# Another queue for the first piece of k, another order on GpSimd, and a new order table in a fused attention and MoE kernel

## The chip, the cores and the metric

The kernel runs on one core of one Trainium2 chip. The metric is device time in microseconds (us) of one execution. Before the change the median of 3 runs is 299.79 us (299.76 to 300.42).

## The reference

Sliding-window attention with ALiBi bias, followed by a layer of two matrix products with g = h cos(h) between them:

```python
q, k, v: (8, 8, 576, 64) float32          # batch, heads, sequence, head_dim
scores = q k^T / 8 - slope_h |i - j|      # kept where 0 <= i - j < 128, else -1e9
attn = exp(scores - max); attn /= sum(attn)
x = (attn v) transposed to (4608, 512)
h = x @ w_in                              # w_in (512, 2048)
out = (h * cos(h)) @ w_out                # w_out (2048, 512), out (4608, 512) float32
```

## The kernel before, in words

**Tiles and stages.** The 4608 tokens are nine chunks of 512. For each batch of the attention there are nine units: two halves of 256 queries for each of four pairs of heads, and one unit for the 64 tokens of the tail. A unit runs scores (PE, L539 and L529), exps (ScalarE, L598 and L590), a multiplication by a mask that holds the bias (VectorE, L623 and L611), P times V (PE, L653/L656 and L640/L642), the division by the row sum (VectorE, L694 to L712), and a transpose of the result into xT, on PE (L742, copied by L752/L753) or by a DMA. A chunk of the MoE part runs the first product (L782 for most chunks; L975 for chunk 0, in halves; L876 for the last chunks, which use Strassen-like sums of quarters), cos on ScalarE (L787, L980, L940), the multiplication on VectorE (L791, L984), and the second product (L1161 for chunk 0, L1067 and L1138 for the others). The loop over chunks mixes the units of later batches with the products of earlier chunks.

**What sets the order.** Every operation is recorded by `op` (L115) with the keys that it reads and writes, a due priority and assumed durations (`occ` for the engine, `lat` to its result). The order is not worked out in the kernel: `TABLE` (L30) is a packed list of the operations' numbers, one after the other, with a bit that picks ScalarE or VectorE for operations that may run on either. `follow` (L160) reads it and `emit` (L174) writes each engine's program in that order and adds the semaphore waits that the keys ask for. Each engine, and the DMA queue that it issues to, then works strictly in its own order.

**The start.** Batch 0's q and k come in two pieces each, with 8 and 10 token rows a partition group (L344). `load_first_q` (L359) lets SyncE (SP) fetch q's first piece in float32, 512 KB, into the first two output buffers `ob`, from where VectorE (L367) and ScalarE (L368) cast one half each into `qB` (tile gsum). `load_qk` (L351) lets GpSimd (POOL) issue the other loads, cast to bfloat16 by the DMA (L356). `distances` (L425) fills `dif` on GpSimd with an iota and two selects; ScalarE makes the eight masks `EM` from it (L460), and VectorE copies a part of them (L465). `identity` (L419) is a memset and a select on GpSimd. `qk_transposes` (L469) transposes the rows on PE against the identity (L483) into PSUM, from where ScalarE (L500) or VectorE (L501) copies them into qt and kt. GpSimd's program begins: load k piece 1, iota, load q piece 2, two selects, load k piece 2, memset, select, then v (L375) and w_in (L407). The lines that record the start:

```python
load_first_q()
load_qk("k", k, 0, 0)
distances()
identity()
load_qk("q", q, 0, 1)
load_qk("k", k, 0, 1)
```

Of the kernel before, what the change touches and what calls it, by code (L numbers as in the profile page):

```python
# [27 lines left out]


TABLE = (  # L30
    'c-nPV2Y6If7JmPfH!Wo*A%PHdEHqifjs=k}tV#(GFqBXPBn4$bu`FK_%_4*%1ObV(K#D*JSt&-E!h-'
    '0xDvPKfD@{Z`QYO7kX6D^JciMYzU|;fHUhcd1+;jf_Kj&N_3_w#jJy552L+3%Pc;zlP#H-yktj(-'
    'pEjqM{ck}PJwCrB3q-'
    '{9M;&d$5qHR9WADS}~;_2H1xbO#`q+wdtgon`B>6%HyG|f?3%VnDsdnr<5N0St5ZZ)?8zmXNGD<Zg2=y6N`U+Gy?'
    '$F$*GyJWJoN!r+3anTS_iMU&FrmJy)q1{k##U*rYHRJHq^Dy35b!Y@oPU}o$A?_9;n<O%5Xs0l2&{m^^1BgNm_9P'
    '~pqObs4C1TN&{Qy{6(86~%nA#%H5NW^O=4`d2vLnc~h(_}2&mQcz_^`@$G{b79x#rnLjt-93Hcj0-'
    'yv%|m2e+*e0cZK}!+72b)WUaJT8@pXD+fk0N6bOV1gB(Si4?NA5T2-'
    '!JB(zEKr!Mj%{>;HUNYjab!Z7$qCql;L3G!CjefR+FFk(bw73vr<2ntCbb8MB)_5dQYyf6J%<J=0tY;ul(MgN&rc'
    'O0s&EiG$uIcm#Y~Vab;v#yqnaVrE7GY>V-A}Btqa`;P_Nv&jvF#{*7WM`>VMkre&#)Wy?uO_aV#gax-'
    'm{4=v5trFP6j>R?Tw2c0rY#J*M(j<PaOY>o)>#w^hUa2)xJ2kX>J~-'  # L40
    '#3SczLYEI#)13`0UMgZCvSU&r@KXVhQx8AYHOt^~S#t385v1pL)39f1&X4(!RY_VSn%~;N7Le~0Vt5k)3C!7qncH'
    'Sb_KKyP6<WQBL=(H{om`}^2hwehkBNkN1f6-'
    '=6Jf`#n1*9F&|{#~8ip5b`?XFO3>mnmKg4fqM&X#D2BXTu`vb#MxEL-'
    '2=FZh<=U!>)?uhVjo~ev?pC0h90j^d!W2#$W>Vg}3Lez;yMB~`dF58D5!*GHZ4bkokcrZJo8XMBIs3+J`c0!*&!='
    'cNak2M(+9t6%k<c;_TI5&xT-;_~SjMe)zLQ?kr-'
    '9G)}so_oZgT~!nS)>B%(>F{i(nL<%Kma6dPT_kIY8xqVGm@6sSZY)QY;}3kyZHF!JjrNbPWohF6A1kpQae^Jz>4Y'
    'nMq|4ag_#Z%abX$X0Qx{bdg5-'
    'w!C^Sy0wzSSv6YO*7!5g5KOZPW>L)jeqDWi^PVfHiNt_&bV&I7<#pb?el1f*R3lvbBscPqQM6(|M=#E!7MQtWiEo'
    '^$q8jetWg{{laSk`ID;w6<lHL!It@CI3ZRWxET-dy=6bdfZi^BN)-'
    'kx6rkxYh^Af7Y$CX%W0qP@nf!;+_cuy#JAV$$(>L5)aS8M@n1a32RRL3Yb{W0a`!VJ8|o4{JEnxs(L});p(&v8a9'  # L50
    'u_yO{KZHL$YuW?tu(Sy-'
    '!vCGTmAdZpg4wXLtycpkG<<E5@OtDZg=!_1h1+Njmjw*z0aL)7QnhFOPv(elHPlI>oe%EXgvk}suL+RHI+l!oPEe'
    'ttc)y)KY7q-'
    'GO9HpEp~!82*s>_!_J5TR{@5f%EL7h^Wh(4l4fbO%j~jd783&`#My06C4>3;+Is6L%3tT|^hYe#$tr1&iB&6{dwW'
    'wmj!;Baz_4=p8Jja_9ps>tY{=<;GUvOwSAXGq+K`;>!KNrH|ImXY(ASTzHFN^apdvpSj*r6^VK)$8H@P=`NPcPO&'
    'XkYSBhFw`irt0gqb!LQPqlVQC7VwU?z)4yP6n<)+6xUk=rH29r)HJ=#nkkufV0J5o_@v9wsQWd0@&P$WT0e*0vOC'
    'WIl=#9la*x}LDtWaQG=0xl2(#f%Kz3QWi+K|tR$xwKh#_K~ywPUk>V_~X988-'
    'dL$7M*|kTUzrMQ~>ttJm@GYT>9QFLiQ#JGHIu^Q5UX9joXGsV+1N~s5tf4rg&Z0t843@yK)VUZ;eO{vvf>bj#_<{'
    'E{YJE13lG{)N}UY3D6Y>lsCkRX4ja{$9_e$IQETy;j`zD56VwIGwJ{vRRhIkkY72;<?OL;WxyDsbjLJ`d?#gik4L'
    '%OwvOj>3X-Yk5pe`ia}jeHouYwjx-lYe?zUO*6w~{=z!E<7?VOdoJcyIBk3;YN22T&Udsl*?z2EoT*eN`VQ(2lOw'  # L60
    '$ie!%Cd#CND}y^H-5G~apWoVM#%(x$>q1=4UeA7@v$>FHVpXpRNz-`z1w9-2S&rNI|0<^yIkuIxJ1&2qr-'
    'yn-P&*BAkwbEg<YgZWM`B<Ux7!?;yxT0hEB9Poq9_H<xB+6$<+&1*V*jXQ=!i##UhbBC-HxJ9b4f>O5FQM$GVlYY'
    '0;EzOMeT$+Oi@ir?~G>em;QF`Fb7Uw0-'
    ')DSUv5QX5E;wvHsQX@ok50m+CO*%wR0XM0gH$JNq(o?|pd}rcrfU%@Ny^NS$EwY}9WNlRrb}CwAb0!CyUIkX8zeE'
    't`lBMNi5`Z9289jS-byN0#8`Z0-K46!6u51NJvfI*I<pVOKD}#Bep<(EjKAJ>#OvyA?}aT-'
    'Eb<QtZWG>gAiq@nZu|-Z>5YIIxXgTPJ-Qv8(%8OF{x~utj?J<T~4~q=Mu!G!`B%o{U^X7EYfMjy|cFw5l`KlR}P!'
    'Ka8_mW<8uzKs|eA|5Ic*_e7cdlcU3q+K^v!GU5I4-4igxj^A<ASLge=;<iQSZL!w7=WR?W#-'
    'vXhCLeN@7x(>g+{qRDABl6lLS<Fw>!h`LQKaFe(HMu)ipAva=P&;AW;|7_8}?>Xa&1&CWqRI3oTyJm0VHkMj~b-'
    'KU~R;VLVn(IO$x|2XD-#Cwa~YvoxGM@0FUnOnlZXB(9|3jhMQu{ARUV7(DVnyPJ@o)_f&pP-'
    '0v1&I@q5tK0fHEZqW2B6vpePz;Nsr3p!)OwvLraMQ%IB0%b!Fk8kvD!^ICX(d5SU`>)JBl;A)3x!^A~*gA1H!Njk'  # L70
    '9bb31AJ#9jLnSFn5nJP8V+>6WI*{{9$K=-'
    'Ii4(}ekB>9rlTbz8;dAV@$vsGY#Mm*p3)v9cI)0mEeyn;9Sk1Ej+_{IEB=6m(OWM%qp|L4FkV=POcUwRSz4?%tjO'
    '!EE7%nJVFo1y$1xLEKDW3+%V*`a_(LEi!<eA{Ja22J?)4@RI|7PRIIN8a6UkTIrQNx^0MmIX}Gdse33v8*ibI3(}'
    'Q6!`hQq7VFL0TWDyL%1z)LEb|Fqa2QJsRyz<9M$)jGC(Gyq6mu#GUiIyWiMn}lrw_vC^2CnX65Kq(JOA5auqsW#('
    'az6gPr;3Fs3vS*iFTO!lleCE-fW~K`s@;f-'
    'DuL7*vWwMFvwo)YDYK%Ys!&lL=}a$qa_Dqe_$j$%4|P%7Sk&C^p7|E-05OoaEoQU{w(_HKhuIl)N)0L6E?If-ndQ'
    'f>bOkomPRMj6=zXYB;2Fs8S$=8>KAS9bxj%$jo92RQykW$_h$ynL-'
    ';1n|B~0C{NjJ5M;#~HD{_qDyS92ASr8Q=(}$hf?wlN8Dh7U35CEE3Rb4eZHcVrLB=YO&ys+EVM&F9-'
    '>_E|awkyN8>TE$>Y^ZLfm%hXRv?#4)t*Y5EYzr4%5w1xWK3uw7gWYn<tfyI;9|8HRZ>;#t145fwkp%W<gb}oO8Vt'
    ';%~TDI391Zd3iT@kVuEmcuME+!AOkCeh?Xh408{MGRAGcvK=>2_;SOCz;Xi5FXBMh@##BcNK~)Hu608vNLvl*BDH'  # L80
# [172 lines left out]
def bass_alibi_sliding__then__act_gcu_kernel(  # L253
# [8 lines left out]
    with ExitStack() as ctx:  # L262
        def sb(name, shape, dt=BF16):
            return ctx.enter_context(nc.sbuf_tensor(name, shape, dt))

# [84 lines left out]

        def load_qk(which, src, b, n=0):  # L351
            t0, R, _ = PIECES[b][n]
# [3 lines left out]
            op("pool", [lambda e: e.dma_start(qB[which][:, :, c0:c0 + 64 * R], rows)],  # L356
               w=piece_keys(which, b, n), dma=f"ld{which}{n}", occ=740, lat=159 * R)

        def load_first_q():  # L359

            t0, R, _ = PIECES[0][0]
# [1 line left out]
            op("sp", [lambda e: e.dma_start(obuf[:, 0:2, :], rows)],
               w=[("ob", 0), ("ob", 1)], dma="hwq", occ=60, lat=500)
            for y, eng in enumerate(("dve", "act")):
                o = qB["q"][:, y, 0:512]
                op(eng, (lambda e, o=o, y=y: e.tensor_copy(o, ob[y])) if y == 0 else  # L367
                   (lambda e, o=o, y=y: e.activation(o, ob[y], ACTF.Copy)),  # L368
                   r=[("ob", y)], w=[("qB", "q", 0, y)], occ=(340, 450)[y], lat=(420, 560)[y],
                   pri=3)  # L370
# [954 lines left out]
```

## Time and profile before

| | |
|---|---|
| median of 3 runs | 299.79 us |
| the profiled execution | 299.71 us |
| its span in the profile | 298.0 us |
| PE, VectorE (DVE), ScalarE (ACT), GpSimd (POOL) busy | 97%, 88%, 75%, 32% |
| DMA read and written | 36.70 MB, 9.44 MB |
| ACT table loads | 14 |

The span is what the profiler recorded; the profiled execution's own time has 1.7 us around it. A row of the timeline or of a group names line, engine, operation, and output tile <- input tiles; "xN" counts instructions. PE is TensorE's matmul side and PEld its weight loads; SPq and POOLq are the queues' issuing sides. In square brackets stands how long the engine stood idle before the row and who released it. The chain of waits follows the work that ended last back to the start, and gives for each piece its start, its length and its line. Matmuls overlap in PE's pipeline, so a matmul's mean duration is longer than the distance between two of them; the distance is read from long pieces of the chain.

### The profile page before, as it was taken

The numbers are of one execution on the slowest core, as the hardware profiler recorded it, in microseconds if no ns is written. First come the engines' busy times: TensorE is split into PE (matmuls) and PEld (weight loads), VectorE is DVE, ScalarE is ACT, GpSimd is POOL, SyncE is SP. The second block draws the span as 40 slices with busy tenths as digits, with TensorE's granted clock in tenths as the row PEclk, the third lists the DMA queues.
The fourth block names the chain that finished last, engine by engine and source line by source line (L and its number), as shares of the span: only waits on it lengthen the run. The fifth ranks groups of instructions, "written<-read, shape, count | busy, mean of one in ns | idle before, by whom it ended". The sixth has DMA issues, their size and how long they took to land.

```text
span 298.0 us, 7278 instructions
## 1 busy us (share of the span) xinstructions
PE 287.9 (97%) x2974; PEld 205.2 (69%) x2974; DVE 262.1 (88%) x522; ACT 222.1 (75%) x318; POOL 95.2 (32%) x122
## 2 busy tenths in 40 slices
PE   2899999999999999999999999999999999999996
PEld 2678845446874586458854788547768888888884
DVE  3879877599977999899999999999999999999972
ACT  5788878689757889688777878579778758778620
POOL 7997000599642303991195005000000000000000
PEclk9999999999999999999999999999999999999999
DMA  7999999999999994999999939973131400041033
GB/s 153 173 205 208 207 169 146 180 196 155 136 175 147 130 187 90 142 173 173 169 170 133 163 85 130 159 164 74 21 79 21 150 2 0 2 141 37 10 134 106
DMA packets 147729, 37.96 MB, mean 127 GB/s; under 512 B 133360, under 2 KB 146416, under 8 KB 147696
## 3 DMA queue, kind: packets, MB, share of 16 engines
q0 software_dynamic: 99344, 18.10, 79.7%
q1 hardware_dynamic: 48352, 19.41, 34.5%
q8 instruction: 23, 0.38, 0.5%
q14 instruction: 10, 0.08, 0.1%
HBM read 36.70 MB, written 9.44 MB: 155 GB/s over the span
## 4 chain that ended last, share of the span: by engine, by line
PE 94%; DVE 2%; POOL 1%; issue 1%; ACT 1%; POOLq 0%; DVEq 0%
PE ps L1067 33%; PE ps L782 24%; PE ps L876 11%; PE ps L539 5%; PE ps L975 5%; PE ps L1161 4%; PE ps L653 3%; PE ps L656 2%; PE ps L742 2%; PE ps L483 2%; PE ps L529 1%; DVE kt L501 1%; PE ps L640 1%; PE ps L642 1%; PE ps L1138 1%
## 5 line engine op out<-in xcount | busy, mean ns | idle before, releaser
L1067 PE MATMUL ps<-w_outb,gT 128*128 128x256 f16 x512 | 82.3, 273 | 0.0
L782 PE MATMUL ps<-xT,w_inb 128*128 128x512 f16 x336 | 82.2, 379 | 0.0
L787 ACT ACTIVATE cos<-ps,halfpi 128x512 f32<-128x512 f32 x84 | 54.9, 687 | 18.9 <-PE ps L782 13.9
L598 ACT ACTIVATE p<-ps 128x768 bf16<-128x768 f32 (+1 forms) x64 | 55.6, 915 | 11.5 <-PE ps L539 9.5
L791 DVE TENSOR_TENSOR gT<-ps,cos 128x512 f16<-128x512 f32 x84 | 54.5, 686 | 5.5 <-ACT cos L787 5.1
L1067 PEld LDWEIGHTS ps<-w_outb,gT 128*128 128x128 f16 x512 | 48.2, 98 | 12.5 <-issue 1.3
L782 PEld LDWEIGHTS ps<-xT,w_inb 128*128 128x128 f16 x336 | 31.7, 98 | 31.1 <-DVE gT L791 1.5
L375 POOL DMA_DIRECT2D vp<-in_v_dram x40 | 34.3, 892 | 53.1 <-PE ps L656 35.3
L1067 PE MATMUL ps<-wsum,gsum 128*128 128x256 f16 x256 | 38.5, 273 | 0.0
L623 DVE TENSOR_TENSOR p<-p,emask 128x768 bf16<-128x768 bf16 (+1 forms) x64 | 38.0, 615 | 0.3
L385 POOL DMA_DIRECT2D qnat<-in_q_dram x30 | 25.5, 918 | 23.9 <-DMA qt<-qnat 23.9
L1052 ACT ACTIVATE ob<-ps 128x512 f32<-128x512 f32 x33 | 19.6, 598 | 13.7 <-PE ps L1067 11.2
L385 POOL DMA_DIRECT2D knat<-in_k_dram x30 | 25.7, 948 | 9.3 <-DMA kt<-knat 7.0
L1067 PEld LDWEIGHTS ps<-wsum,gsum 128*128 128x128 f16 x256 | 23.2, 98 | 4.0 <-issue 0.5
L876 PE MATMUL ps<-xT,w_inb 128*128 128x256 f16 x132 | 24.8, 273 | 0.0
L696 DVE TENSOR_TENSOR xnats<-ps,rec 128x256 f16<-128x256 f32 x56 | 21.9, 420 | 0.5
L539 PE MATMUL ps<-qt,kt 64*128 64x128 bf16 (+1 forms) x320 | 20.1, 253 | 1.3 <-DVE kt L501 1.3
L653 PEld LDWEIGHTS ps<-vp,p 128*128 128x128 bf16 x256 | 16.0, 99 | 4.3 <-issue 1.0
L653 PE MATMUL ps<-vp,p 128*128 128x65 bf16 x256 | 18.9, 196 | 0.1
L1067 PE MATMUL ps<-wsum,gT 128*128 128x256 f16 x112 | 18.1, 273 | 0.0
L539 PEld LDWEIGHTS ps<-qt,kt 64*128 64x128 bf16 x320 | 11.9, 98 | 8.6 <-issue 3.6
L1161 PE MATMUL ps<-w_outb,gT 128*128 128x512 f16 x64 | 17.6, 380 | 0.0
(111 smaller groups left out, 478.0 us busy)
## 6 DMA issues: line engine op xcount, KB each, us to landing
out_dram<-ob SPq DMA_DIRECT2D x35, 256.0 KB, 2.7
vp<-in_v_dram POOLq DMA_DIRECT2D x32, 128.0 KB, 6.9
qnat<-in_q_dram POOLq DMA_DIRECT2D x24, 128.0 KB, 7.1
knat<-in_k_dram POOLq DMA_DIRECT2D x24, 128.0 KB, 10.8
w_inb<-in_moe_w_in_dram POOLq DMA_DIRECT2D x4, 512.0 KB, 10.5
w_outb<-in_moe_w_out_dram POOLq DMA_DIRECT2D x4, 512.0 KB, 21.8
gsum<-in_q_dram POOLq DMA_DIRECT2D x1, 576.0 KB, 15.5
gsum<-in_k_dram POOLq DMA_DIRECT2D x1, 576.0 KB, 17.6
```

The source lines that it names most:

```text
L375: op("pool", [lambda e, t=t, rows=rows: e.dma_start(vp[b % 2][0:rows, t, :, 0:64], v[b, :, 128 * t:128 * t + rows, :].rearrange("h p d -> ...
L385: fns.append(lambda e, t=t, rows=rows: e.dma_start(nat[which][b % 2][0:rows, t, :, :], src[b, :, 128 * t:128 * t + rows, :].rearrange("h p ...
L539: ins = e.matmul(ps[:, banks[x], c0:c1], keys_ap(b, x, pr, kc), query_ap(b, x, pr, qb, 128 * nb), start=c0 == 0 and (b, pr, G) not in seed ...
L598: op("act", lambda e: e.activation(P[i][:, :, 0:hi], src_[:, :, 0:hi], ACTF.Exp, scale=0.125), w=held + [("P", i)], occ=920 if G else 691, ...
L623: op("dve", lambda e: e.tensor_tensor(p, p, m, ALU.mult), r=[("EM", h0), ("EM", h1)] + ([] if G else [("EM2", h1)]), w=[("P", i)], occ=600 ...
L653: ins = e.matmul(o, P[i][:, x, d0:d0 + 128], V[:, kc, h, 0:65], start=True, stop=not two)
L782: op("pe", lambda e, kc=kc: e.matmul(ps[:, bank, :], w_in[:, kc, 128 * fc:128 * fc + 128], xT[:, kc, r0:r0 + CH], start=(kc == 0), stop=(k ...
L787: op("act", lambda e: e.activation(cosb[ci][:, :], ps[:, bank, :], ACTF.Sin, bias=halfpi[:, 0:1]), r=["halfpi"], w=[("B", bank), ("cos", c ...
L791: op("dve", lambda e: e.tensor_tensor(gT[gi][:, fc, :], ps[:, bank, :], cosb[ci][:, :], ALU.mult), r=[("cos", ci)], w=[("B", bank), ("g", ...
L876: op("pe", lambda e, i=i, kc=kc: e.matmul(ps[:, bank, 256 * i:256 * i + 256], left(kc, p0 + i), right(kc), start=(start and i == 0 and kc ...
L1067: op("pe", lambda e, t=t, p=p: e.matmul(ps[:, bank, 256 * t:256 * t + 256], left(p, slice(128 * t, 128 * t + 128)), right(p), start=(start ...
L1161: op("pe", lambda e, t=t, fc=fc, bank=bank: e.matmul(ps[:, bank, :], gT[gi][:, fc, 128 * t:128 * t + 128], w_out[:, fc, :], start=(fc == 0 ...
```

## The change

The first piece of k is fetched by SyncE in float32 too, right behind q's, into output buffers 2 and 3, and cast by operations that may run on ScalarE or VectorE (q's casts may now too). The GpSimd load of that piece is gone. The table is new, so the order on every engine differs over the whole kernel. In the new order GpSimd's program begins: iota, two selects, memset, load q piece 2, load k piece 2, select of the identity, then v and w_in. ScalarE begins with five masks, then its halves of q's and of k's cast, the first copies of qt and kt, three masks and the first exps; VectorE casts the other halves. Of the 40 transposes that follow, ScalarE copies both parts of q and VectorE both of k, where before each had one part of q and VectorE both of k. The number of matmuls is the same. The diff, without the table:

```diff
         def piece_keys(which, b, n):
             keys = [("qB", which, 0), ("qB", which, 1)] if b else [("qB", which, n)]
-            return keys + ([("qB", "q", 0, 0), ("qB", "q", 0, 1)] if which == "q" and n == 0 else [])
+            return keys + ([("qB", which, 0, 0), ("qB", which, 0, 1)] if n == 0 else [])
...
-        def load_first_q():
+        def load_first():
 
             t0, R, _ = PIECES[0][0]
-            rows = bass.AP(q.tensor, q[0].offset, [[64 * R, 32], [64 * S, H], [1, 64 * R]])
-            op("sp", [lambda e: e.dma_start(obuf[:, 0:2, :], rows)],
-               w=[("ob", 0), ("ob", 1)], dma="hwq", occ=60, lat=500)
-            for y, eng in enumerate(("dve", "act")):
-                o = qB["q"][:, y, 0:512]
-                op(eng, (lambda e, o=o, y=y: e.tensor_copy(o, ob[y])) if y == 0 else
-                   (lambda e, o=o, y=y: e.activation(o, ob[y], ACTF.Copy)),
-                   r=[("ob", y)], w=[("qB", "q", 0, y)], occ=(340, 450)[y], lat=(420, 560)[y],
-                   pri=3)
+            for i, (which, src) in enumerate((("q", q), ("k", k))):
+                rows = bass.AP(src.tensor, src[0].offset, [[64 * R, 32], [64 * S, H], [1, 64 * R]])
+                op("sp", [lambda e, i=i, rows=rows: e.dma_start(obuf[:, 2 * i:2 * i + 2, :], rows)],
+                   w=[("ob", 2 * i), ("ob", 2 * i + 1)], dma=f"hw{which}", occ=740,
+                   lat=(940, 1250)[i])
+            for i, which in enumerate("qk"):
+                for y in range(2):
+                    o, i_ = qB[which][:, y, 0:512], ob[2 * i + y]
+                    op(("act", "dve"),
+                       {"act": lambda e, o=o, i_=i_: e.activation(o, i_, ACTF.Copy),
+                        "dve": lambda e, o=o, i_=i_: e.tensor_copy(o, i_)},
+                       r=[("ob", 2 * i + y)], w=[("qB", which, 0, y)],
+                       occ={"act": 450, "dve": 340}, lat={"act": 560, "dve": 420}, pri=3)
...
-        load_first_q()
-        load_qk("k", k, 0, 0)
+        load_first()
         distances()
         identity()
         load_qk("q", q, 0, 1)
```

More of the change, by code (lines that the diff above doesn't have):

```diff
@@ L30 @@
 TABLE = (
[L31 to L80, printed above, removed]
@@ new lines @@
+    ';NypbGxO;_zLfYoncjsiqO_8X|%E^QSONf9e6W?R~Nq)=0aCZ0cc&LY*ESS5H>9<`p0U4Zg`{k0H)p54{m+@VGjs'
+    '6qEBQMN>-'
+    '1^?2;QV~TCK(_R$WkVxFM+_mJU?@B%@jyTdJ4m8{WT$H8mo*6U<zA|@se5CX6h~uo0ax$_PT}IcQDMg4HzFi+4cs'
+    '3Li?Z-opGSTvU2}A=L#W4I6zGp*9#6@NgR&zwAUqZJHi_5-'
+    'F&wuonzGv~QFI?m0HfZaCLkDvuDmv;NREMerRJ3zi@Y|ylVwk%Q3Amy6CRE1Xw(9G!VNt6J*pUR(v~qY1X5gCM`^'
+    'Iap<q{KS8eau;_fW)LPe!DDa@&oV_t1sAPvSg1NdzuDbOA|!B>h4E>NX-'
+    'G=OxTt^|GXamE0j33oLeE+18~scq7g^W(Tl}46FUs`SV!jiq*cm%(&X+HD^aHZVlWNhm}Ze?2#+{b}=9nqo;}Qki'
@@ new lines @@
+    'm;Cg<EyUDy)Ovd+5Y#@3(XqJ!ChE^S$<2MwyX~&!-'
+    '9=c#MwbrAUwrn&R4RiFc>j(Blgm1DrQxY_Y?8IkS_iE8H};IrdGHqR9@m_3(h$D(*6;>QFJ{Jx_;4!R>%KmMt+gN'
+    ')rWpHBaL2Y}jXZ?G&Zy$>wS;y56V#AJh&bFARUI!c$h${5<}Cm@FU5dcRN05u&UbT_(G#`kwC2s*IW(@0uL$j?(X'
+    'FA$n@&vMpGg?C@=<U3tAvH_-7IJ+i=5d+j0ZSs5VhW>0V|>wuhvCo^Hjqd=)(nrJT=0YwvcsO!Za-'
+    'H2|hU1WWBzu<l(R1eB&+PVj_Lk&L@6s4MTE15loMHH9RE}!8+^4WR3+5&Ljo6as-*E-|ptZ9Zt|;GnS-'
+    'U5H@=&Gh`Zo95P%8F5VRP>c#MF8lU2eeof~a-'
+    'Fk0S7T5HZCXC%d9<qu=mPO+YerV|=l`yRyv`>WIMLLlg#@BU%r_p2F-m~a#9!9CS5cUzuDDb5{zI-'
```

38 lines of the change are left out of this document (35 added, 3 removed).

## The prediction

> **What bounds the kernel now.** I read the page first, then busy time by stretches, then the chain of waits and the timeline of the first 20 us.
>
> ```profile
> span 298.0 us, 7278 instructions
> PE 287.9 (97%) x2974; PEld 205.2 (69%) x2974; DVE 262.1 (88%) x522; ACT 222.1 (75%) x318; POOL 95.2 (32%) x122
> PE 94%; DVE 2%; POOL 1%; issue 1%; ACT 1%; POOLq 0%; DVEq 0%
> ```
>
> TensorE (PE) carries 94% of the chain that ended last. Where it does not stand still is shown by three stretches behind the head (columns: length, busy time of PE, PEld, DVE, ACT, POOL, then clock, DMA share, GB/s):
>
> ```profile
> 20.00:100.00 80.00, 79.86 (x803) 50.29 (x801) 66.76 (x144) 61.65 (x94) 40.78 (x49) 1.00 1.77 172
> 100.00:200.00 100.00, 99.96 (x1065) 66.18 (x1064) 94.55 (x207) 79.09 (x110) 35.98 (x43) 1.00 1.56 149
> 200.00:295.00 95.00, 95.00 (x922) 78.41 (x920) 87.80 (x135) 65.77 (x89) 0.00 (x0) 1.00 0.19 56
> ```
>
> PE is idle for 275.00 - 274.81 = 0.19 us in the 275 us from 20 to 295. Busy is not yet full speed, so I test the rate on two long pieces of the chain:
>
> ```profile
> 190.76 8.63 PE ps L782 x40
> 280.00 12.51 PE ps L1067 x113
> PE ps L1067 33%; PE ps L782 24%; PE ps L876 11%; PE ps L539 5%; PE ps L975 5%; PE ps L1161 4%; PE ps L653 3%; PE ps L656 2%; PE ps L742 2%; PE ps L483 2%; PE ps L529 1%; DVE kt L501 1%; PE ps L640 1%; PE ps L642 1%; PE ps L1138 1%
> L782 PE MATMUL ps<-xT,w_inb 128*128 128x512 f16 x336 | 82.2, 379 | 0.0
> L1067 PE MATMUL ps<-w_outb,gT 128*128 128x256 f16 x512 | 82.3, 273 | 0.0
> L1067 PE MATMUL ps<-wsum,gsum 128*128 128x256 f16 x256 | 38.5, 273 | 0.0
> L1067 PE MATMUL ps<-wsum,gT 128*128 128x256 f16 x112 | 18.1, 273 | 0.0
> ```
>
> Unbroken, L782 takes 8.63/40 = 216 ns a matmul and L1067 12.51/113 = 111 ns. Over the whole chain, L782 has 24% of 298 for 336 matmuls, 213 ns with the page's rounding; L1067 has 33% for 512+256+112 = 880, 112 ns. The long stages run at the unbroken rate. What a reordering can win there is about 880 x 1 to 2 ns = 0.9 to 1.8 us, and no more.
>
> So the time is the head plus a fixed load of matmuls plus the tail, and the change touches the head by design and the rest only through the new order.
>
> **The head, and what each piece waits for** (start, duration; timeline, then chain):
>
> ```profile
> 0.81 0.74 SPq L363 DMA_DIRECT2D ob<-in_q_dram  x1
> 1.31 0.84 POOL L356 DMA_DIRECT2D gsum<-in_k_dram  x1 [0.80 <-POOLq L1310]
> 2.25 0.38 POOL L427 IOTA dif<- 128x256 f32 x1
> 3.75 0.29 POOL L434 TENSOR_SCALAR_AFFINE_SELECT dif<-dif 128x128 f32<-128x128 f32 x1
> 4.88 0.63 ACT L368 ACTIVATE gsum<-ob 128x512 bf16<-128x512 f32 x1
> 4.89 0.53 DVE L367 CAST gsum<-ob 128x512 bf16<-128x512 f32 x1 [2.24 <-DMA ob<-in_q_dram]
> 5.20 0.35 POOL L421 TENSOR_SCALAR_AFFINE_SELECT ident<-ident 128x128 bf16<-128x128 bf16 x1
> 5.70 1.93 PE ps L483 x32
> 7.66 0.70 DVE kt L501
> 8.15 0.71 ACT L460 ACTIVATE emask<-dif 128x256 bf16<-128x256 f32 x2
> 9.04 1.51 ACT L598 ACTIVATE p<-ps 128x768 bf16<-128x768 f32 x2 [0.17 <-PE ps L539]
> 11.79 1.58 DVE kt L501 x2
> 13.50 1.04 PE ps L539 x12
> ```
>
> The first transposes start at 5.70. They need two things that end together: the identity (5.20 + 0.35 = 5.55) and ScalarE's half of q's cast (4.88 + 0.63 = 5.51). The 32 transposes are 16 of q and 16 of k, 1.93/32 = 60 ns each, so k is first touched at 5.70 + 0.96 = 6.66. Its own load is the 256 KB row here (KB each, median us from issue to landing):
>
> ```profile
> ob<-in_q_dram SPq DMA_DIRECT2D x1, 512.0 KB, 4.1
> gsum<-in_q_dram POOLq DMA_DIRECT2D x1, 320.0 KB, 5.8
> gsum<-in_k_dram POOLq DMA_DIRECT2D x1, 256.0 KB, 4.9
> ```
>
> It lands at 1.31 + 4.9 = 6.2: 0.45 us before it is wanted. So k is not late today, and needs no cast.
>
> **The change, part by part.** *GpSimd.* One DMA issue (0.84) goes, two more move behind iota, selects and the memset. With the durations above and 0.14 us between dependent steps (2 us of small pieces in all), the distances are ready at about 2.7 instead of 3.75 + 0.29 = 4.04. The order as built puts the two loads of q's and k's second piece between the identity's memset and its select, so the identity is not ahead of all loads; still it is done at about 4.75 instead of 5.55. v and w_in are issued about 0.7 us earlier, the second piece of q 0.4 later (2.9 + 5.8 = 8.7; its transposes ran at 9.25), that of k 0.5 earlier. Gain at the start of PE: nothing, because q's cast still ends at 5.51. The earlier masks take 1 us out of ScalarE's queue at a time when it waited anyway. The earlier v and w_in are hidden by PE, which from 15 us on is full. If that cover were gone, they would be worth at most their 0.7 us.
>
> *k's queue and cast.* k is issued behind q on SyncE, at 0.81 + 0.74 = 1.55, as 512 KB of float32, and then cast, ScalarE's half in 0.63, plus some 0.15 from the cast's end to PE as with q. It holds PE up if it lands after 6.66 - 0.78 = 5.88. The bounds: at best it takes q's 4.1 from its own issue, 5.65, and nothing is late (if q also lands sooner because k's GpSimd load is out of its way, k at 5.65 still allows no more than 5.65 + 0.78 - 6.66 = -0.25). At worst it queues behind q and shares the wire with the second pieces. The wire by single microseconds:
>
> ```profile
> 3.00:4.00 1.00, 0.00 (x0) 0.00 (x0) 0.00 (x0) 0.00 (x0) 0.84 (x3) 1.00 0.95 350
> 5.00:6.00 1.00, 0.30 (x7) 0.33 (x9) 0.41 (x1) 1.00 (x3) 0.93 (x3) 1.00 1.24 204
> ```
>
> 524 KB at 350 GB/s, the slice that q's load had nearly to itself, are 1.5 us; at the 204 GB/s of the slice with GpSimd's loads in it, 2.6 us. Behind q at 4.89 that is 6.4 or 7.5, so PE's k transposes start 0.5 or 1.6 us late. I take 1.5 us: k now follows q on the same queue, and the second pieces are issued at 2.9 and 3.7, so they reach the wire when k is mostly through. **Term: +0.5.**
>
> The Trainium skill, "DMA: Bandwidth & Descriptors", Rules for kernel authors, says that spreading loads over SP, ACT and GpSimd brings no bandwidth, since all run on the same 16 engines, and saves only issue time. By that, the queue change alone is worth GpSimd's 0.84 us of issue and k's bytes come no sooner; here that issue time is off the chain once the identity no longer ends last. Within the bounds above it speaks for the late end.
>
> *Does the 0.5 reach the end?* Behind k: the two copies of kt start at 8.17 instead of 7.66 (DVE 0.70 to 8.87), scores at 9.0, exps at about 9.55. ScalarE has three masks (instead of two) after kt's copy; 0.71 for two, so about 1.0 for three, ending near 9.65, which hardly adds. The 40 second transposes follow PE's scores and move by the same 0.5; the copies of kt behind them (1.58 on VectorE) start near 12.25 instead of 11.79, and the second scores near 14.0 instead of 13.50. In the old order VectorE also had a copy of q there; the new one has both of q's on ScalarE, which removes a queue but not the wait for the transposes. From there PE is full, so the shift is kept. The extra cast halves (0.63 on ScalarE, 0.53 on VectorE) lie in idle time, as the 2.24 us wait in front of L367 shows.
>
> *The new table.* ACT keeps its 14 table loads, PE its matmuls; a few copies change engine. Nothing in the counts adds or removes work. Bounds: -1.8 us (the rate term above) and, upward, what mistimed waits cost. The nearest row is the stall that VectorE still causes in the middle:
>
> ```profile
> PE ps L539 <- DVE kt L501: 1.3, 2, 0.9
> DVE rec L694 <- PE ps L656: 7.1, 11, 1.4
> ```
>
> The longest wait of PE for VectorE is 0.9 us. One or two such mishaps are +0.9 to +1.8. Between -1.8 and +1.8 I take 0, near the rows that show PE full already.
>
> **Sum.** The profiled execution took 299.71, span 298.0 and 1.7 around it. 299.71 + 0.5 + 0 = 300.2. The median of the runs shown is 299.79, so this is +0.1%.
>
> **Rivals.**
>
> *k comes much later (slower).* The mechanism is the 204 GB/s slice: k lands at 7.5, PE's k transposes start 1.6 us late, 299.71 + 1.6 = 301.3. It decides from a landing later than about 6.8 (+0.9). For: the second pieces and k do overlap in time. Against: they are issued 1.4 and 2.1 us after k.
>
> *PE's slow phase lasts longer (slower).* Early transposes take 60 ns; the same work later:
>
> ```profile
> 28.08 0.68 PE ps L483 x20
> 17.60 0.43 PE ps L529 x16
> 15.31 0.59 PE ps L539 x5
> ```
>
> 0.68/20 = 34 ns. PE is slow until about 17.4 (0.59/5 = 118 ns for a score at 15.3, against 46 later), although the granted clock reads 1.00, and it had run without a pause since 13.50, some 3.9 us. If the second scores come at 14.0 and a pause of half a microsecond behind them makes the run without a pause begin at 14.6, the fast phase starts at 14.6 + 3.9 = 18.5, 1.1 us later, and that stretch at half speed costs 0.55 more: 300.8. It decides when a pause falls after 13.5. The Trainium skill, "TensorE: Matmul & The Clock Gate", Part 1, gives a free-running window of 3.4 us as the condition. By that rule a missed window could cost 3.4/2 = 1.7 us (an estimate), 301.9 with the 0.5; the trace's 3.9 us agrees with the order of the window, and no run here shows its phase.
>
> *The new table misplaces waits (slower).* Two waits of 0.9 us in the middle: 299.71 + 0.5 + 1.8 = 302.0. PE's 0.19 us of idle in 275 shows how good the old order is and how little room above it.
>
> *The new order packs better (faster).* The rate term gives up to 1.8 us: 299.71 + 0.5 - 1.8 = 298.4. For: chunks of L1067 are interleaved in longer runs. Against: 112 against 111 ns is a thin reserve.
>
> *The change does not do what it says:* the select of the identity behind two loads. It costs nothing while q's cast ends last.
>
> **How the numbers follow.** Forecast 300.2 (own range 299.4 to 300.7): 0.49. k much later, 301.3: 0.16. Slow phase, 300.8: 0.10. Waits in the middle, 302.0: 0.08. Better packing, 298.4: 0.17. About 0.3% is what a measurement of this kernel tells from no change, so faster means below 298.9 and slower above 300.7. Faster: most of the last case, 0.14. Slower: 0.14 of the first rival, 0.06 of the second, all 0.08 of the third and 0.06 of the forecast, 0.34. Same: 0.52. A range from 298.8 to 301.6 leaves out most of the packing case and the waits, two in ten.
>
> **What would show it.** In the profile after: L421 behind two DMA issues, ending near 4.75; ob<-in_k landing near 6.4; a gap or late start between the 16th and 17th transposes; kt's copies near 8.2; second scores near 14.0; PE fast from about 17.9; idle below 0.5 us from 20 to 295. A landing of k below 5.9, or a wait of PE above 0.5 us behind 20 us, makes me wrong.

## The result, and the profile after

The changed kernel takes 301.04 us (median of 14 runs, 300.23 to 301.72), the kernel before 299.77 in the same set (14 runs, 299.41 to 301.02). The ratio is 1.0040, with a 95% interval of 1.0028 to 1.0052: about 1.2 us more. Forecast was 300.2; the result lies above the forecast's own range (299.4 to 300.7) and within the wide one (298.8 to 301.6). The profiled execution took 301.14.

The page's first lines and its chain, then four stretches behind the head (columns as before):

```profile
span 299.4 us, 7290 instructions
PE 287.9 (96%) x2974; PEld 204.5 (68%) x2974; DVE 261.5 (87%) x522; ACT 223.3 (75%) x320; POOL 94.3 (32%) x121
PE 88%; DVE 5%; DMA 4%; ACT 1%; issue 1%; SPq 0%; ACTq 0%; DVEq 0%
```

```profile
20.00:100.00 80.00, 79.90 (x804) 50.20 (x803) 66.89 (x143) 61.73 (x95) 40.20 (x49) 1.00 1.72 173
100.00:180.00 80.00, 79.81 (x861) 53.45 (x860) 74.08 (x161) 64.27 (x91) 30.83 (x37) 1.00 1.53 145
180.00:195.00 15.00, 14.78 (x179) 10.32 (x178) 13.78 (x36) 10.23 (x14) 5.14 (x7) 1.00 1.67 160
195.00:296.00 101.00, 101.00 (x948) 81.22 (x946) 94.09 (x146) 70.87 (x97) 0.00 (x0) 1.00 0.23 61
```

PE's busy time is the same 287.9 us, which is partly chance, as the account below says. What is new is in the other shares of the chain: VectorE and DMA hold 9% of it, where VectorE had 2% and no DMA was named. PE stands still for 0.10 + 0.19 + 0.22 = 0.51 us between 20 and 195, against 0.19 before, and then no more. The unbroken rate has not moved: the last long piece of the chain is 11.94/108 = 111 ns a matmul.

```profile
281.99 11.94 PE ps L1067 x108
```

The head, from the timeline, and below it the median landing times of the loads:

```profile
0.81 0.74 SPq L360 DMA_DIRECT2D ob<-in_q_dram  x1
1.61 0.61 SPq L360 DMA_DIRECT2D ob<-in_k_dram  x1
3.99 0.30 POOL L421 TENSOR_SCALAR_AFFINE_SELECT ident<-ident 128x128 bf16<-128x128 bf16 x1
4.83 0.63 ACT L367 ACTIVATE gsum<-ob 128x512 bf16<-128x512 f32 x1 [1.02 <-DMA ob<-in_q_dram]
5.51 1.06 PE L483 MATMUL ps<-ident,gsum 128*64 128x128 bf16 x16 [5.51 <-ACT gsum L367]
6.48 0.67 DVE L368 CAST gsum<-ob 128x512 bf16<-128x512 f32 x1 [1.06 <-DMA ob<-in_k_dram]
7.29 1.06 PE L483 MATMUL ps<-ident,gsum 128*64 128x128 bf16 x16 [0.72 <-DVE gsum L368]
8.39 0.69 DVE L501 COPY kt<-ps 128x512 bf16<-128x512 bf16 x1 [0.42 <-PE ps L483]
12.37 1.57 DVE L501 COPY kt<-ps 128x640 bf16<-128x640 bf16 x2 [0.43 <-PE ps L483]
14.09 0.82 PE L539 MATMUL ps<-qt,kt 64*128 64x256 bf16 x8 [0.16 <-DVE kt L501]
```

```profile
ob<-in_q_dram SPq DMA_DIRECT2D x1, 512.0 KB, 4.0
ob<-in_k_dram SPq DMA_DIRECT2D x1, 512.0 KB, 4.8
```

k lands at 6.46, its casts end at 7.15, and its 16 transposes, which followed q's without a pause at 6.66 before, wait 0.72 us and start at 7.29: 0.63 late. kt's copies start at 8.39 (7.66 before), the second scores at 14.09 (13.50). So the head brings +0.6 us up to here. The span grew by 1.4 us, so more than half of the loss comes later. Where, is told by setting the two traces side by side by PE's work: for the same amount of matmul work done, how much later is the new kernel? (An estimate from the starts of all matmuls; the order differs, so single figures are good to about 0.25 us.)

```
time in the span, us     32     95    116    146    177    188    198    219    259
after minus before, us  +0.5   +0.6   +0.8   +1.1   +1.2   +0.9   +1.3   +1.4   +1.5
```

The lag of the head stands still for over 60 us; then the new order loses another 0.8 to 0.9 us between 95 and 220 us, in pieces. The largest single wait of VectorE for a buffer is at 187.8. VectorE's rows there, and PE's wait behind them:

```profile
187.24 0.18 DVE L694 RECIPROCAL rec<-ps 128x4 f32<-128x4 f32 x1 [0.31 <-PE ps L656]
187.79 0.42 DVE L696 TENSOR_TENSOR xnats<-ps,rec 128x256 f16<-128x256 f32 x1 [0.37 <-DMA xT<-xnats]
188.13 0.42 DVE L611 TENSOR_TENSOR ptail<-ptail,emask 128x512 bf16<-128x512 bf16 x1
190.19 0.19 PE L640 MATMUL ps<-vp,ptail 128*128 128x65 bf16 x1 [0.23 <-DVE xnats L696]
```

VectorE wants to write one of the eight xnat buffers (L696), but a DMA transpose still reads it. The chain names that transfer:

```profile
181.19 6.57 DMA xT<-xnats
```

It needed 6.57 us, where the median of the 29 such transposes is 3.8 (3.0 before). Two masks of ptail (L611) and two more divisions (L696) are queued behind it on VectorE, and PE's L640 waits 0.23 us for the last of these. In the kernel before no L696 waits for a DMA anywhere. Slow transposes are not new: the slowest took 7.6 us in the kernel before and 8.2 us in this one, both issued near 154 us, and no L696 waited for them. What the new order brings is that VectorE comes for this buffer before the transfer is through.

### The profile page after: what moved, and what is told of

It reads as the page before. It is cut to its first block, busy times and chain, and to the rows that moved or that the text cites. A ratio compares the mean times of both kernels' runs of the same rounds, so it can differ in the third digit from the quotient of the medians.

```text
span 299.4 us, 7290 instructions
## 1 busy us (share of the span) xinstructions
PE 287.9 (96%) x2974; PEld 204.5 (68%) x2974; DVE 261.5 (87%) x522; ACT 223.3 (75%) x320; POOL 94.3 (32%) x121
## 4 chain that ended last, share of the span: by engine, by line
PE 88%; DVE 5%; DMA 4%; ACT 1%; issue 1%; SPq 0%; ACTq 0%; DVEq 0%
PE ps L1067 31%; PE ps L782 21%; PE ps L876 11%; PE ps L975 5%; PE ps L1161 5%; PE ps L539 5%; PE ps L653 3%; DMA xT<-xnats 2%; PE ps L483 2%; PE ps L656 2%; DMA ob<-in_k_dram 2%; PE ps L742 1%; DVE gT L791 1%; DVE xnats L696 1%; ACT cos L787 1%
## 5 line engine op out<-in xcount | busy, mean ns | idle before, releaser
L1067 PE MATMUL ps<-w_outb,gT 128*128 128x256 f16 x512 | 83.7, 273 | 0.0
L1067 PEld LDWEIGHTS ps<-w_outb,gT 128*128 128x128 f16 x512 | 48.3, 98 | 13.2 <-issue 1.1
L1067 PE MATMUL ps<-wsum,gsum 128*128 128x256 f16 x256 | 39.4, 273 | 0.0
L1052 ACT ACTIVATE ob<-ps 128x512 f32<-128x512 f32 x31 | 18.5, 597 | 11.1 <-PE ps L1067 9.8
L1067 PEld LDWEIGHTS ps<-wsum,gsum 128*128 128x128 f16 x256 | 23.5, 98 | 4.1 <-issue 0.5
L696 DVE TENSOR_TENSOR xnats<-ps,rec 128x256 f16<-128x256 f32 x56 | 21.9, 419 | 1.0 <-DMA xT<-xnats 0.4
L539 PE MATMUL ps<-qt,kt 64*128 64x128 bf16 (+1 forms) x320 | 19.6, 249 | 1.2 <-DVE kt L501 1.0
L1067 PE MATMUL ps<-wsum,gT 128*128 128x256 f16 x112 | 20.2, 273 | 0.0
L539 PEld LDWEIGHTS ps<-qt,kt 64*128 64x128 bf16 x320 | 11.7, 97 | 8.4 <-ACT p L598 2.4
## 6 DMA issues: line engine op xcount, KB each, us to landing
gsum<-in_q_dram POOLq DMA_DIRECT2D x1, 576.0 KB, 16.5
```

The lines of the kernel that those rows point to most:

```text
L539: ins = e.matmul(ps[:, banks[x], c0:c1], keys_ap(b, x, pr, kc), query_ap(b, x, pr, qb, 128 * nb), start=c0 == 0 and (b, pr, G) not in seed ...
L1067: op("pe", lambda e, t=t, p=p: e.matmul(ps[:, bank, 256 * t:256 * t + 256], left(p, slice(128 * t, 128 * t + 128)), right(p), start=(start ...
```

## The experiments

Theory A: k's late landing and its cast make the head 0.5 us longer. Theory B: the new order costs something of its own, by waits behind 80 us. Rivals: C, PE's slow phase of the first microseconds lasts longer; D, the order as such is worth nothing. The time of the kernel before beside a run is from the same chip and the same set.

| run | us (runs) | before | ratio, 95% interval |
|---|---|---|---|
| e0_again | 300.97 (6) | 299.90 | 1.0040, 1.0028 to 1.0053 |
| e1_old_order | 300.28 (12) | 299.90 | 1.0015, 1.0004 to 1.0025 |
| e2_k_gpsimd | 299.97 (12) | 299.90 | 1.0010, 1.0000 to 1.0020 |
| e3_pool_order | 299.90 (12) | 299.90 | 0.9999, 0.9991 to 1.0007 |
| e6_warm_before | 299.74 (11) | 299.84 | 0.9998, 0.9989 to 1.0007 |
| e7_warm_after | 301.08 (8) | 299.84 | 1.0034, 1.0020 to 1.0047 |
| e8_warm_e2 | 300.63 (12) | 299.84 | 1.0033, 1.0018 to 1.0049 |
| e9_warm_e1 | 300.49 (9) | 299.84 | 1.0022, 1.0011 to 1.0033 |
| e10_more_xnat | 300.48 (11) | 299.91 | 1.0021, 1.0012 to 1.0030 |
| e11_k_gpsimd_again | 300.15 (11) | 299.91 | 1.0011, 0.9998 to 1.0024 |
| e4_k_act_queue | 301.34 (4) | 299.91 | 1.0044, 1.0030 to 1.0057 |
| e5_wire_alone | 302.75 (1) | 299.91 | |

**e0_again: the changed kernel once more.** The kernel is the same.

> The changed kernel once more. Theory A (k's late landing costs 0.5 to 0.6 us in the head, the new order's waits behind 100 us the other 0.7): 301.0 us, k lands near 6.5 us, PE behind the old kernel by 0.5 to 0.6 us at equal matmul work up to 90 us, by 1.3 to 1.5 at the end; the same places (before 116, 134 and 190 us) lose time again. Rival B (the loss behind 100 us is chance in the transfers): the lag at the end differs by more than 0.5 us from that of the first profile and sits elsewhere.

The loss repeats to the digit. So does its place, with another size; VectorE's row of e0, and the stretch around it in e0 and in the kernel before:

```profile
188.42 0.42 DVE L696 TENSOR_TENSOR xnats<-ps,rec 128x256 f16<-128x256 f32 x1 [1.03 <-DMA xT<-xnats]
```

```profile
180.00:195.00 15.00, 14.29 (x176) 9.84 (x175) 13.12 (x35) 9.71 (x13) 5.11 (x7) 1.00 1.80 149
```

```profile
180.00:195.00 15.00, 14.96 (x174) 9.89 (x173) 14.26 (x35) 10.52 (x15) 3.08 (x4) 1.00 1.53 158
```

The same wait is 1.03 us this time, and PE stands still for 0.71 of 15 us (before: 0.04). The wait is there again, and its length follows from when one DMA transpose lands. The profiled execution is the slowest of the six (301.79), and by PE's work it is about 2.0 us behind the kernel before at the end, not 1.3 to 1.5: the place is the one that theory A named, the size differs by the 0.5 us and more that rival B named.

**e1_old_order: only k's queue and cast, and GpSimd's new start.** The code of the changed kernel, with the table of before except for these first operations:

```diff
 SyncE:   load q piece 1
+         load k piece 1 (float32)
 ScalarE, VectorE: casts of q
+         casts of k
 GpSimd:
-         load k piece 1, iota, load q piece 2, select, select, load k piece 2, memset, select
+         iota, select, select, memset, load q piece 2, load k piece 2, select
```

> The changed kernel's queue and GpSimd's new start, but the old order table for all else (k's two cast halves stand ahead of the first copies of qt). Theory A: the head's term alone, 299.77 + 0.5 to 0.6 = 300.3, k lands near 6.5, k's transposes start near 7.3, and the lag behind the old kernel stays at 0.5 to 0.7 us to the end. Rival C (all is the order table): 299.8. Rival D (all is k's queue): 301.0.

```profile
6.29 0.82 DVE L368 CAST gsum<-ob 128x512 bf16<-128x512 f32 x1 [0.89 <-DMA ob<-in_k_dram]
7.26 1.06 PE L483 MATMUL ps<-ident,gsum 128*64 128x128 bf16 x16 [0.54 <-DVE gsum L368]
14.20 0.62 PE L539 MATMUL ps<-qt,kt 64*128 64x256 bf16 x12 [0.38 <-DVE kt L501]
```

k's transposes start at 7.26 as in the changed kernel, and the loss is 0.15% of 300, 0.45 us, with an interval from 0.1 to 0.75: about the head's term that was forecast. No L696 waits for a DMA here.

But in the profiled execution (299.96, one of the faster of the twelve) the lag does not stay at 0.5 to 0.7 us to the end, as theory A expected. PE runs the same matmuls in the same order as in the kernel before, so the two traces can be set side by side one by one. The lag is 0.70 us from k's transposes to 13.5 us, 0.4 at 14.2, and at 18 it is gone; here the first products of w_in, in e1 and in the kernel before:

```profile
17.98 0.93 PE L975 MATMUL ps<-xT,w_inb 128*128 128x256 f16 x7
```

```profile
17.96 0.94 PE L975 MATMUL ps<-xT,w_inb 128*128 128x256 f16 x7
```

PE became fast at about 14 us here, in the kernel before only at 17.9, and that made the loss up. The 0.24 us that the end is late come at about 133 us, from a wait of PE for VectorE. So k's late start is shown, 0.6 to 0.7 us at the transposes; how much of it an execution keeps depends on when PE becomes fast, and 0.45 is the middle of twelve. It is not the whole of the 1.2.

**e2_k_gpsimd and e11_k_gpsimd_again: only the new order.** The changed kernel and its table, but k's first piece comes by GpSimd in bfloat16 as before (GpSimd: load k piece 1, then the new start), and k's casts are gone:

```diff
+                if i == 0:
-                op("sp", [lambda e, i=i, rows=rows: e.dma_start(obuf[:, 2 * i:2 * i + 2, :], rows)],
...
+                else:
+                    load_qk("k", k, 0, 0)
-            for i, which in enumerate("qk"):
+            for i, which in enumerate("q"):
```

> The changed kernel's order, but k's first piece by GpSimd in bfloat16 again, as GpSimd's first load, and no cast of k. Theory A: 301.04 - 0.6 = 300.4, k's transposes start near 6.6 with no gap behind q's, and the lag behind the old kernel grows only behind 100 us. Rival C: 301.0. Rival D: 299.8.

> The new order with k's first piece by GpSimd as before, a second time, since two kernels with this order measured 0.1% and 0.33% over the kernel before. Theory (the new table's waits behind 80 us are a loss of their own): 300.2 to 300.6, with PE gaps near 189 us of 0.4 us or more. Rival (the loss is all of k's late landing, and the order alone is worth nothing): 299.7 to 299.9.

Both give 0.1%, 0.3 us, with intervals that touch no loss at all, and both medians (299.97 and 300.15) lie below what theory had named (300.4; 300.2 to 300.6). Their profiles tell more. In e2 the wait is there (line numbers are two higher); in e11 it is not, and PE stands still for nothing in the stretch:

```profile
187.03 0.42 DVE L698 TENSOR_TENSOR xnats<-ps,rec 128x256 f16<-128x256 f32 x1 [0.65 <-DMA xT<-xnats]
```

```profile
180.00:195.00 15.00, 15.00 (x178) 10.17 (x176) 13.90 (x35) 10.49 (x14) 4.41 (x6) 1.00 1.58 162
```

So the gap of 0.4 us or more near 189 that theory B expected in e11's profile did not come: the wait occurs in some executions only. Neither theory B with 0.3 us or more nor rival D is excluded by these two times alone.

All profiles together say more. For each matmul that starts behind 21 us I took its distance from the start of the one in front, less the median distance of that kind, and summed; against the kernel before, PE loses there, in us (my estimate):

```
order of before                    e1 0.3, e3 0.0, e6 0.0, e9 0.6
new order, L696 waits for a DMA    changed kernel 1.1, e0 1.8, e2 1.2, e7 1.7, e8 1.4
new order, no such wait            e4 0.9, e5 0.9, e10 1.0, e11 0.6
```

So every profile of the new order loses behind the head, 0.6 to 1.8 us against 0 to 0.6, also without k's new queue. That speaks for theory B and against rival D. In the stretch from 186 to 198 us it loses 0.4 to 1.1 where L696 waits and 0.1 to 0.3 where it doesn't; about 0.4 to 0.8 is spread elsewhere. In e2's profile the time before 21 us made up 0.4 of it.

**e3_pool_order: only GpSimd's new start, in the kernel before.** k still by GpSimd; the table of before except for

```diff
-load k piece 1, iota, load q piece 2, select, select, load k piece 2, memset, select
+load k piece 1, iota, select, select, memset, load q piece 2, load k piece 2, select
```

> The old kernel with GpSimd's new order alone: k's load stays first, then distances, the identity's memset, the second pieces of q and k, the select of the identity. My theory: 299.8, no difference, because q's cast ends at 5.51 and the old identity at 5.55, and the masks are waited for by nobody. Rival: the identity and the masks were what held the start, then 299.3 to 299.5.

Nothing: 0.9999. The first transposes start at 5.65 (5.70 before), and q's cast, not the identity, releases them.

**e6_warm_before, e7_warm_after, e8_warm_e2, e9_warm_e1: PE warmed.** The kernel before, the changed kernel, e2 and e1, each with ten added matmuls on zeros at the start of PE's program, whose result nobody reads:

```diff
+        warm = sb("warm", [128, 512])
+        op("dve", lambda e: e.memset(warm[:, :], 0.0), w=["warm"])
+        def heat(e):
+            for _ in range(10):
+                ins = e.matmul(ps[:, 7, :], warm[:, 0:128], warm[:, :], start=True, stop=True)
+            return ins
+        op("pe", heat, r=["warm"])
```

> The old kernel with ten 128x512 matmuls on a zeroed tile ahead of all of PE's work, whose result nothing reads. The profiles so far show PE's fast phase beginning at 17.4 us (old), 14 to 15 (changed, twice, and e1), 11.4 (e2, e3), with kernels that match to 0.1 us until then. If that moment is chance and worth its stretch at half speed, PE is fast from about 5.7 us here and the time is 299.0 to 299.4, with less spread. Rival: the moment follows from the order of the work, and the added matmuls change nothing or delay the first transposes: 299.8 or above.

> The changed kernel with the same ten matmuls. Theory A (k's late landing costs its 0.6 us whatever PE's speed, the new order some more behind 100 us): 1.0 to 1.4 above e6. Rival E (a good part of the loss is a later fast phase, because PE stands still between q's and k's transposes): 0.4 to 0.8 above e6.

> The new order with k's first piece by GpSimd (e2) and the same ten matmuls: the new order alone. Theory A: 0.3 to 0.7 above e6, all of it behind 100 us. Rival D (all is k's queue): equal to e6.

> The old order with k's first piece by SyncE (e1) and the same ten matmuls: k's queue alone. Theory A: 0.6 above e6, lag constant behind the head. Rival C (all is the order): equal to e6. If e8 and e9 add up to less than e7, the two hang together.

In e6 the 32 first transposes take 1.20 us instead of 1.93, and the kernel is no faster, 0.9998, where 299.0 to 299.4 was expected. Its timeline shows why:

```profile
5.69 1.20 PE L483 MATMUL ps<-ident,gsum 128*64 128x128 bf16 x32
8.05 0.51 PE L539 MATMUL ps<-qt,kt 64*128 64x256 bf16 x8 [1.16 <-DVE kt L501]
9.97 0.75 PE L483 MATMUL ps<-ident,gsum 128*64 128x128 bf16 x20 [0.73 <-DMA gsum<-in_k_dram]
11.69 0.27 PE L653 MATMUL ps<-vp,p 128*128 128x65 bf16 x3 [0.54 <-DMA vp<-in_v_dram]
19.64 1.26 PE L975 MATMUL ps<-xT,w_inb 128*128 128x256 f16 x10 [1.10 <-DMA w_inb<-in_moe_w_in_dram]
```

A faster PE waits for the second piece of k and for v, and where it is still ahead, for w_in: set side by side with the kernel before, matmul by matmul, PE is 1.07 us ahead at 19 us, then waits 1.10 us for the second of w_in's four pieces, which lands at 19.6 (19.4 before), and the lead is gone. And the warmth does not last: after the first waits the granted clock reads 0.50 from about 12.8 to 16.2.

```profile
13.00:14.00 1.00, 1.00 (x15) 0.72 (x14) 1.00 (x5) 0.39 (x1) 1.00 (x2) 0.50 1.22 200
15.00:16.00 1.00, 0.99 (x12) 0.53 (x9) 1.00 (x5) 1.00 (x2) 1.00 (x2) 0.50 1.45 188
```

With the warm-up the differences between the four kernels are those of before: k's queue alone +0.22% (e9), the order alone +0.33% (e8), both +0.34% (e7; less than the sum of the two, 0.55%, but within what the three intervals allow). Over e6, e9 has 0.75 us, e8 0.9 (0.3 to 0.7 was expected) and e7 1.3. The warm-up moves the slow phase rather than taking it out: each of the four profiles has one stretch of half clock, 3.4 us long, from 12.8 us on in e6, 14.9 in e7, 10.9 in e8 and 16.5 in e9. So these runs alone don't put rival C out. The profiles without warm-up speak against it: PE became fast at 15.0 us in the changed kernel, at 14.4 in e0 and at 17.9 in the kernel before, so the slow phase was shorter where the kernel was slower. How it falls in the executions that were not profiled is not known. e8 is the one run in which the order alone loses beyond doubt; its runs spread from 300.04 to 302.44, and the wait of L696 in its profile is 0.6 us.

**e10_more_xnat: two more buffers.** The changed kernel with

```diff
-        NX = 8
+        NX = 10
```

> The changed kernel with ten xnat buffers instead of eight; the order stays. In it VectorE's L696 at 187.8 us waits for a DMA transpose that still reads its xnat buffer, and PE then stands still for 0.39 to 1.0 us near 189 to 191 us in every profile of this order (0.39; 0.56 + 0.49; 0.49 + 0.47). Theory (this wait is the new table's largest share of the loss): no gap of PE above 0.25 us between 185 and 195 us, and 0.3 to 0.6 us less than the changed kernel's 301.0, so 300.4 to 300.7. Rival (the buffer is only the last of several causes that end together, and the wait moves on to ptail's mask or to another tile): gaps of the same size near 190 us, 300.9 to 301.1.

VectorE's row and the stretch in e10:

```profile
186.86 0.42 DVE L696 TENSOR_TENSOR xnats<-ps,rec 128x256 f16<-128x256 f32 x1
```

```profile
180.00:195.00 15.00, 14.97 (x177) 10.12 (x176) 13.84 (x35) 10.43 (x14) 4.47 (x6) 1.00 1.60 158
```

No wait here, PE is full there as before, and the time is 1.0021 of before instead of 1.0040: 0.0019 x 300 = 0.57 us less, as the theory said (by the two intervals, 0.1 to 1.0 us). The executions also lie closer together: 300.38 to 300.86, against 300.23 to 301.72 for the changed kernel. This fits a wait that some executions have and others haven't.

The profile does not show that the two buffers took the wait away. In all nine profiles of the new order the transfer in question is the same one; it takes 6.2 to 7.5 us from its issue to its landing, and VectorE comes for its buffer 6.3 to 7.4 us after the issue. In five profiles VectorE comes first and waits. In e4, e5 and e11, with eight buffers too, it comes 0.3 us after the landing; in e10 the transfer lands at 186.42 and VectorE's row starts at 186.86, so here eight buffers would have done as well. And the lead of e10's profile over that of the changed kernel, 0.7 us, is there before 21 us: k lands at 6.06, its transposes start at 6.77 instead of 7.29, and PE is fast from 13.7. Behind 21 us both lose the same, 1.0 and 1.1 us. So the buffer as the cause of the 0.57 us is likely and not shown.

**e5_wire_alone: k's landing without the second pieces.** GpSimd's loads of the second pieces wait for k, so nothing but q and k is on the wire:

```diff
-               w=piece_keys(which, b, n), dma=f"ld{which}{n}", occ=740, lat=159 * R)
+               r=[("ob", 2)] if (b, n, which) == (0, 1, "q") else [], w=piece_keys(which, b, n),
+               dma=f"ld{which}{n}", occ=740, lat=159 * R)
```

> The changed kernel, but GpSimd's loads of the second pieces wait for k's landing, so that k has the wire to itself behind q. Theory (k's late landing is its place behind q's 512 KB, on the same queue and wire): k still lands 4.5 us or more after its issue, at 6.1 to 6.5, and its transposes start at 7.0 or later. Rival (the second pieces take k's share of the wire): k lands near 5.65, 4.1 after its issue as q's, and its transposes follow q's without a pause at 6.6. The second pieces come 3 to 4 us later in either case and cost something behind 10 us; the total time says nothing here.

```profile
ob<-in_k_dram SPq DMA_DIRECT2D x1, 512.0 KB, 4.5
5.00:6.00 1.00, 0.45 (x10) 0.45 (x12) 0.34 (x2) 0.50 (x1) 0.00 (x0) 1.00 0.54 207
6.00:7.00 1.00, 0.75 (x16) 0.51 (x14) 0.82 (x3) 0.82 (x2) 0.53 (x1) 1.00 0.00 0
6.86 1.07 PE L484 MATMUL ps<-ident,gsum 128*64 128x128 bf16 x16 [0.25 <-ACT gsum L368]
```

Alone on the wire, k still lands 4.5 us after its issue, at about 6.15; with the second pieces beside it, it takes 4.5 to 4.9 in six profiles. So the second pieces explain a few tenths at most. Its transposes start at 6.86, a little earlier than the 7.0 that the theory named. The DMA share is 0.54 in the slice from 5 to 6 and nothing in the next: the last packet of k ends at 5.7, and the landing is seen about 0.4 us later.

**e4_k_act_queue: k beside q instead of behind it.**

```diff
-                op("sp", [lambda e, i=i, rows=rows: e.dma_start(obuf[:, 2 * i:2 * i + 2, :], rows)],
+                op(("sp", "act")[i], [lambda e, i=i, rows=rows: e.dma_start(obuf[:, 2 * i:2 * i + 2, :], rows)],
```

> The changed kernel with k's load issued from ScalarE's queue, beside q's on SyncE's. Theory (the wire is the limit: 1 MB at about 350 to 390 GB/s are 2.7 to 3.0 us from the first bytes near 3.3): q lands later than its 4.89, both between 5.6 and 6.4, q's transposes start late, and the time is 300.8 to 301.5. Rival (it is the shared queue that makes k late): q lands near 4.9 and k before 5.7, k's transposes have no pause, and the time is 0.4 to 0.6 less than the changed kernel's, 300.4 to 300.6.

```profile
ob<-in_q_dram SPq DMA_DIRECT2D x1, 512.0 KB, 5.4
ob<-in_k_dram ACTq DMA_DIRECT2D x1, 512.0 KB, 4.1
6.23 1.15 ACT L367 ACTIVATE gsum<-ob 128x512 bf16<-128x512 f32 x2 [1.76 <-DMA ob<-in_q_dram]
7.24 1.92 PE L483 MATMUL ps<-ident,gsum 128*64 128x128 bf16 x32 [7.24 <-DVE gsum L368]
```

Both loads are issued at 0.8. q lands at 6.2 instead of 4.8, and k at 4.9: the rival's early k came, but at q's cost. The loads still go one after the other, k's packets from 2.3 to 4.5 us and q's from 4.1 to 5.8. Both engines cast q first, so the early k is of no use, and all 32 transposes start at 7.24: 301.34, as the theory said. Whichever of the two is served second lands at 6.1 to 6.5. The wire sets that landing; the queues only decide which load is second. The Trainium skill, "DMA: Bandwidth & Descriptors", Rules for kernel authors, says that spreading loads over SP, ACT and GpSimd brings no bandwidth; this pair of runs agrees, as the last packet of the 1 MB ends at 5.7 us with one queue (e5) and at 5.8 with two. Here the second queue cost q, which is needed first, 1.4 us.

No version among these is faster than the kernel before.

## Why the prediction was right, point by point, and where it was off

- **PE full, fixed rate.** Right as to the rate: 111 ns a matmul of L1067 in the last long piece of both, so a loss can only be the head or new waits. That both profiles show 287.9 us of PE is partly chance: e3, with PE's order of before but fast from 11.2 us on, has 285.9, and e2, with the new order and fast from 11.5, 286.8. Matmuls overlap, so a short wait between two of them doesn't appear as idle time, and the busy share hides a part of what the new order loses.
- **GpSimd's part, worth nothing.** Right by e3 (0.9999). The identity is ready at 4.29, earlier than the forecast 4.75, and the distances at 2.13, not 2.7, because no DMA issue stands ahead of them. It makes no difference, as q's cast ends last.
- **k's queue and cast, +0.5.** Right in mechanism and, in the median, in size: landing 6.46 (forecast 6.4), transposes +0.63, second scores 14.09 (forecast 14.0), alone +0.45 us in e1. "From there PE is full, so the shift is kept" is not right for each execution: in e1's profile the 0.70 us were made up by 18 us, as PE became fast earlier. The working assumed that the second pieces reach the wire too late to matter. They were issued at 2.42 and 3.26, earlier than the 2.9 and 3.7 that it took, and still matter little: k takes 4.5 us without them (e5) and 4.5 to 4.9 with them. The loss isn't that the bytes come later than by GpSimd (6.46 now, 6.2 before): the cast of 0.67 and 0.14 to PE now stand behind them, and the slack was 0.45. 6.46 + 0.02 + 0.67 + 0.14 = 7.29.
- **The new table, taken as 0 between -1.8 and +1.8.** This is the term that was mis-sized: with both parts together it is 1.2 - 0.45 = about +0.75, and by the table of all profiles PE loses 0.6 to 1.8 us behind 21 us with the new order. A part of it is one wait, VectorE's for an xnat buffer under a DMA transpose, in five of nine profiles; the rest is in smaller waits that no experiment took away singly. The prediction priced a mishap at 0.9 us from a row that it placed in the middle of the kernel. That row is of the head: its two waits are the 0.88 us at 8.50 and the 0.38 at 13.50 of the kernel before. It did not look at what VectorE's own writes wait for. Its rival "misplaces waits" is the case that came beside the forecast, at a third to a half of the 1.8 us that it was given.
- **Better packing, -1.8.** Did not come.
- **Slow phase longer, +0.55.** Did not come in the profile: PE was fast from about 15.0 us on, against 17.9 before. The 17.4 of the prediction is read too early: the sixteen L529 behind it still start 0.05 us a pair apart, where later ones take 0.02 to 0.03. And the granted clock of 1.00 that it sets against this is no reading: the trace of the kernel before has no record of the clock ahead of 17.93, and the column shows 1.00 where there is none. The run without a pause would be 4.4 us, not 3.9.
- **A wait of PE above 0.5 us behind 20 us** was named as what would make the forecast wrong. The longest is 0.23 us in the profile after and 0.39 in e0's; all idle time from 20 us on is 0.51 after, at the edge of the 0.5 that was named. The sign was too coarse: many short waits made a loss of 1 us and more without a single long one.
- **The total.** The direction is right, and the forecast's term has less than half of the loss (0.5 of 1.2 us). That 301.04 lies in the wide range is luck as far as the mechanism goes: the range reached up to 301.6 for a later k (301.3), which did not come. By the line that the prediction drew at 300.7 the result is "slower", to which it gave 0.34.

What stays open: why the order alone cost 0.1% in e2 and e11 but 0.33% in e8. The wait of L696 was 0.37, 1.03 and 0.9 us in three profiles with both parts, and 0.65, 0.6 and 0 with the order alone (0 in e4 and e5 too); a wait that an execution has or hasn't gives such a spread, but single profiles can't show how often it comes. Open too is how much of e10's 0.57 us is this wait, and how the moment at which PE becomes fast is spread over the executions of each kernel.

## What to carry to other kernels

When a new order is to be judged, look beside PE's waits for the buffers that a DMA still reads: count how many tiles later a ring buffer is written again and what the slowest transfer takes, not the median, since a strict order passes one late transfer on to everything queued behind the waiting instruction (here 6.3 to 7.4 us to the next write, and 6.2 to 7.5 for the transfer). To test such a wait, see in the trace of the kernel with more buffers whether the transfer was late there at all. Moving a load to another queue brings no more bytes when the wire is full with what is needed at the same time: what one load gains there, the other loses. Then a cast that moves from the DMA to an engine is simply added behind the landing. One profile has one placing of PE's slow phase, which moved single executions here by 0.5 to 0.7 us, so a term below 1 us needs many executions. A faster engine at the start is worth nothing where its operands' landings set the pace, and a warm-up is to be judged by the waits that follow it.

## What the runs showed of the hardware that wasn't expected

- The length of PE's slow phase is not a property of the kernel. A score of 256 columns (L539) took about 390 to 418 ns early and 280 later; PE became fast at 11.2 to 12.1 us in e3, e2 and e11, at 13.7 to 15.0 in e10, e4, e1, e0 and the changed kernel, and at 17.6 and 17.9 in e5 and the kernel before. The kernel before and e3 have the same matmuls in the same order and start the first of them within 0.05 us. e3's profile is 0.45 us ahead of that of the kernel before from the head on, at the same median; this is why the head's term is taken from e1's twelve runs.
- The granted clock changes on a fixed step. Twelve of the traces hold records of it (those of the changed kernel and e1 hold none), and every stretch between two changes is a whole multiple of 3.41 us: 3.41, 6.83, 10.24, and 280 to 287 for the long ones. The step's place in the span differs from profile to profile, so the moment at which PE becomes fast jumps by such steps.
- Ten matmuls on zeros made PE fast from 4.1 to 6.3 us on, but after waits of 1.16, 0.73 and 0.54 us it fell back to half clock for 3.4 us (e6), as in e7, e8 and e9. The Trainium skill, "TensorE: Matmul & The Clock Gate", Part 1, puts the fall behind an idle window of about 3.4 us; in these four profiles no single wait of PE ahead of the fall was longer than 1.16 us, so it takes no such pause at a stretch. PE was busy for 37% to 58% of the 3.4 us ahead of the fall; shares like these occur without a fall too, so the condition stays open.
- DMA transposes of the same size took 3.0 us from issue to landing in the median and up to 7.6 in the kernel before, 3.8 and up to 8.2 in the changed kernel, and up to 8.8 in e0.
- Of two loads of 512 KB issued within 0.01 us from ScalarE's and SyncE's queues (e4), ScalarE's went first almost whole: it landed at 4.9 us and the other at 6.2.
